# A fused scan and feed-forward kernel: one weight transfer issued earlier, w_in's later pieces converted in another order

## The chip, the cores and the metric

The kernel runs on one core of one Trainium2 chip. The metric is device time of one execution in microseconds (us). The kernel before takes 349.14 us, the median of three runs (349.01 to 349.2).

## What is computed

A chunked state-space scan (Mamba-2) on 4 batches, 8 heads, 768 positions, head size 32 and state size 16; its output, reshaped to 3072 tokens of 256 values, goes through a feed-forward block of width 2048 with the quick GELU:

```python
for c in range(nc):                      # chunks of the sequence, per batch and head
    cum = np.cumsum(log(a)[chunk])
    y[chunk] = (C @ B.T * exp(cum_i - cum_j) * causal) @ x   # within the chunk
             + (C @ state) * exp(cum)                        # from the chunks before
    state = exp(sum(log a)) * state + (B * exp(cum_end - cum)).T @ x
h = y.reshape(3072, 256) @ w_in          # 256 x 2048
g = h / (1 + exp(-1.702 * h))
out = g @ w_out                          # 2048 x 256
```

x, a, B and C are 32-bit numbers. w_in and w_out arrive in 64-bit floating point and are converted on the chip, from their bits.

## The kernel before, in words

The tokens are worked off in six groups of 512 (`g` 0 to 5). A group has two pairs of chunks (pairs 0 and 1 for group 0, 2 and 3 for group 1). For group 0 the plain products are used: 16 calls of `hidden(0, f)`, f = 0 to 15, each two products on TensorE of w_in's block f with yT (the scan's output turned, halves k = 0 and 1) into one bank of PSUM `h`, and one Silu on ScalarE that reads the bank into gT. Then `project_all(0)` runs f = 0 to 15 again, two products each of w_out's block f with gT into the banks `o`. From group 1 on the products are made with a seven-product scheme (lines L948, L958, L1053, L1060) whose steps are written out by hand; the change does not touch it.

The order on each engine is the order in which the program calls the helpers (`in_order`, L21, keeps it). While group 0 is in `hidden` and `project_all`, the lists `in_hidden[0]` and `in_project[0]` (L1221 to L1253) name, for a place f, what is emitted right behind `hidden(0, f)`, or ahead of f in `project_all`. So place 8 of `in_hidden[0]` stands behind the Silu of f = 8 on ScalarE, and ahead of that of f = 9.

**The weights' way.** They come in ten pieces (`PIECES`, L154): pieces 0 to 3 hold two blocks of w_in each, pieces 4 and 5 four blocks each (8 to 11 and 12 to 15), pieces 6 to 9 four blocks of w_out each. A piece is transferred by `fetch` (two DMAs on SP's queue) into one of four buffers `bits`; pieces 0 and 1 share a buffer, 2 and 3 too. It is converted in four steps:

- `fields(i)`: two VectorE instructions (L192, L195) cut exponent (`p`, written p2 in the code) and mantissa (`m`) out of the upper words,
- `clamp(i)`: two ScalarE instructions (L203, L204) on `p`, which need the first of `fields`,
- `rounded(i)`: one VectorE instruction (L208) adds the lower words to `m`,
- `join(i, parts)`: two VectorE instructions per part (L222, which needs `clamp`, and L228), the last of which writes w_in or w_out.

`narrow(i)` emits rounded(i), fields(i + 1), join(i), all on VectorE. `join` also fetches a later piece: behind piece 1 comes piece 6, behind piece 5 piece 9 (`NEXT`).

**Beside it** VectorE, ScalarE and TensorE prepare the scan of pairs 2 and 3. `store_a` at place 5 clips the decays az on VectorE (L353, L357, L358) and stores them. `pick_a` at place 6 makes X from az by two ScalarE instructions (L366). `fan_all` at place 9 spreads X by 16 small products into PSUM and then runs four VectorE scans (L450) and two products Be (L461); with it a bank `rows4` is written (L501, L530), which `since_fanned` reads on VectorE (L541, L543). The banks of `h`, `rows4`, the turned B and C (`tp`) and `o` come from one pool of four, so a product waits until the bank's last reader is done. In `project_all`, places 0 and 2 turn B and C of pairs 2 and 3 (`turn`, L597, L590, and CsT, L667); place 9 makes scores, state increments (`gain`, L713) and states; `finish` adds the part of the earlier states (`inter`, L824, at place 13) and the part within the chunk (`intra`, L838, at place 15) into PSUM and copies it to yT of group 1 (L871).

**The start.** SP issues a, B, piece 0 and the four DMAs of x for pairs 0 and 1. Piece 1 is held: GpSimd writes one element of its buffer (L171) after it has made CsT of pair 0, and SP's queue waits for that. Pieces 1 to 5 and az follow on SP's queue. A ninth DMA waits for the landing of the one eight earlier (eight semaphores are used in turn). `finish(range(PG))` runs the 128 products `intra` of pairs 0 and 1, a filling product `dense(4)`, then `inter` by halves t, each followed by its two ScalarE copies to yT (L856).

Of the kernel before, what the change touches and what calls it, by code (L numbers as in the profile page):

```python
# [35 lines left out]
def kernel(  # L36
# [31 lines left out]
    nc = tc.nc  # L68
# [69 lines left out]
    def load(p, parts=None):  # L138
        if parts is None:
            parts = "bcx" if p < 2 * PG else "bx"  # L140
            if p >= 2 * PG:
                load_blocks(p)
        for part in parts:
            dst, src, e = {"b": (rb, B, N), "c": (rc, C, N), "x": (rx, x, D)}[part]
            dst[p] = raw.tile([P, 2, NH, e], FP32, tag=part, name=f"{part}{p}",
                              bufs=2 if part == "c" else 3)
            for k in range(2):
                b, c = divmod(2 * p + k, NC)
                sl = slice(c * P, (c + 1) * P)
                nc.sync.dma_start(out=dst[p][:, k], in_=src[b, :, sl, :].rearrange("h s d -> s h d"))  # L150
# [55 lines left out]
    def rounded(i):  # L206

        nc.vector.scalar_tensor_tensor(out=mantissa[i].bitcast(FP32), in0=bits[i][0],  # L208
                                       scalar=2.0 ** -32, in1=mantissa[i],
                                       op0=ALU.mult, op1=ALU.add)  # L210
# [4 lines left out]
    def join(i, parts=1):  # L215

        name, f, n = PIECES[i]
        n //= parts
        low, m, p2 = bits.pop(i)[1], mantissa.pop(i), power.pop(i)
        for k in range(parts):  # L220
            cols, fs = slice(k * n * DM, (k + 1) * n * DM), slice(f + k * n, f + (k + 1) * n)
            nc.vector.scalar_tensor_tensor(out=p2[:, cols], in0=low[:, cols], scalar=0x80000000,  # L222
                                           in1=p2[:, cols], op0=ALU.bitwise_and, op1=ALU.bitwise_or)
            if name == "in":
                dst, h = w_in[:, fs].rearrange("p f k e -> p (f k e)").unsqueeze(1), 1
            else:
                dst, h = w_out[:, :, fs].rearrange("p c f e -> p c (f e)"), 2
            nc.vector.scalar_tensor_tensor(  # L228
                out=dst, in0=m[:, cols].bitcast(FP32).rearrange("p (h e) -> p h e", h=h),
                scalar=2.0 ** -20, in1=p2[:, cols].bitcast(FP32).rearrange("p (h e) -> p h e", h=h),  # L230
                op0=ALU.mult, op1=ALU.mult)
        for n in NEXT.get(i, ()):
            fetch(n)

    def narrow(i):
        rounded(i)
        if i + 1 < len(PIECES):
            fields(i + 1)
        join(i, 2 if i == 4 else 1)


    scratch = dram.tile([NC, 2, NB * NH, H], FP32, name="scratch")
# [47 lines left out]
    fetch(0)  # L290
    load(0, "x")
    load(1, "x")


    edge = const.tile([P, 2], FP32, name="edge")
# [84 lines left out]
    for i, n, head in ((0, 1, PG), (1, 2, PG), (0, 0, 1)):  # L380
        t = whose[32 * i:32 * i + 32, n:n + 1]
# [202 lines left out]
    def area(name):  # L584
        return psa.tile([P, R, 4 * P], FP32, tag="cb", name=name)
# [202 lines left out]
    def finish(pairs, steps=range(2)):  # L788


        g, first = divmod(pairs[0], PG)
        early = pairs[0] < PG

        swap = g > 2
        if 0 in steps:
            if early:
                y = [bank(f"y0_{i}")[:, :2 * P].rearrange("p (k i) -> p k i", i=H) for i in range(4)]
                begun_y[0] = [[y[2 * t + i] for t in range(NK)] for i in range(2)], set()
            else:
                both = area(f"y{pairs[0]}")[:, :, :len(pairs) * 2 * H].rearrange(  # L800
                    "p (s t) (k i) -> p s t k i", s=2, i=H)
                begun_y[pairs[0]] = [[both[:, i, t] for t in range(NK)] for i in range(2)] + [both], set()
        y, begun = begun_y[pairs[0]]

        def begin(i, t, parts):
            new = not begun & {(i, t, q) for q in parts}
            begun.update((i, t, q) for q in parts)
            return new

        def inter(n, p, ts=range(2)):  # L810

            for k in range(2):
                for i in range(2):
                    m = 2 * k + i
                    if (4 * p + m) % (2 * NC) == 0:
                        continue
                    old = state[p][:, m - 1] if m else state[p - 1][:, 3]
                    for r in range(R):
                        t = r // 2
                        if t not in ts:  # L820
                            continue
                        half = r % 2 ^ (swap and i)
                        rows, to = slice(32 * r, 32 * r + 32), Q * D * half
                        nc.tensor.matmul(  # L824
                            out=y[i][t][to:to + Q * D, 2 * n + k], lhsT=old[rows],
                            rhs=st[p]["CsT"][rows, k, SIDES[i]],
                            start=begin(i, t, range(Q * half, Q * half + Q)), stop=early,
                            tile_position=(32 * r, to), skip_group_check=True)

        def intra(n, p):  # L830
            L = Ls[p]
            for k in range(2):
                for h in range(NH):
                    for i, side in enumerate(SIDES):
                        t, q = divmod(h, HB)
                        if i and swap:
                            q = (q + Q) % HB
                        nc.tensor.matmul(  # L838
                            out=y[i][t][D * q:D * q + D, 2 * n + k], lhsT=rx[p][side, k, h],
                            rhs=L[side, k, h // Q, h % Q],  # L840
                            start=begin(i, t, (q,)), stop=not early, tile_position=(H * i, D * q),
                            skip_group_check=True)

        cols = slice(2 * first * P, 2 * (first + len(pairs)) * P)

        if first == 0:
            yT[g] = ffn.tile([P, NK, TG], FP32, tag="yT", name=f"yT{g}")
        if early:
            for n, p in enumerate(pairs):
                intra(n, p)  # L850
            dense(4, area("idle")[:, 0])
            for t in range(NK):
                for n, p in enumerate(pairs):
                    inter(n, p, (t,))
                for i in range(2):
                    nc.scalar.activation(  # L856
                        yT[g][:, t, cols].rearrange("p (k s i) -> p s k i", s=2, i=H)[:, i], y[i][t],
                        AF.Copy)
        else:
            for step in steps:  # L860
                for n, p in enumerate(pairs):
                    (inter, intra)[step](n, p)
            if 1 not in steps:
                return
            o = yT[g][:, :, cols].rearrange("p t (k s i) -> p s t k i", s=2, i=H)
            for i in range(2):
                if i and swap:
                    for to, src in (SIDES, SIDES[::-1]):
                        nc.scalar.activation(o[to, i], y[2][src, i], AF.Copy)
                else:  # L870
                    nc.scalar.activation(o[:, i], y[2][:, i], AF.Copy)  # L871
        for p in pairs:
            state.pop(p - 1, None)
            st.pop(p)
            Ls.pop(p)
# [287 lines left out]
    def dense(n, t):  # L1163
        nc.tensor.matmul(out=t[:, :n * H], lhsT=ones,
                         rhs=ones[:, :H].unsqueeze(1).to_broadcast([P, n, H]),
                         start=True, stop=True, skip_group_check=True)
# [27 lines left out]
    gain(range(PG))  # L1194
    parts_first()
    since_start(0, nc.gpsimd)
    fetch(1, held=nc.gpsimd)
    for i in range(2, 6):
        fetch(i)
    rows_a(az, (nc.sync,))  # L1200
    since_start(1, nc.gpsimd)
# [2 lines left out]
    dense(8, bank("dense"))  # L1204
    finish(range(PG))
    join(0, 2)
    fields(1)
    clamp(1)
    table(AF.Silu)
    rounded(1)  # L1210
    fold_ident(1)
    join(1)
    fields(2)
    clamp(2)
# [3 lines left out]
    def at(places, i, *work):  # L1218
        places.setdefault(i, []).extend(work)

    in_hidden = [{} for _ in range(NG)]  # L1221
    in_project = [{} for _ in range(NG)]
# [7 lines left out]
    at(in_hidden[0], 6, lambda: pick_a(PG))  # L1230
    at(in_hidden[0], 9, lambda: fan_all(PG))
    at(in_hidden[0], 9, since_fanned)
    for i, k, c in ((2, 1, 1), (3, 2, 2), (4, 4, 4), (5, 6, 8), (6, 9, 12), (7, 12, 15)):
        at(in_hidden[0], k, lambda i=i: narrow(i))
        at(in_hidden[0], c, lambda i=i: clamp(i + 1))
    at(in_hidden[0], 9, lambda: spread(PG + 1), lambda: spread_rows(1))
    n, p = 2 * PG, 3 * PG
    pairs = PG, PG + 1
# [5 lines left out]
    at(in_project[0], 5, lambda: narrow(9))  # L1244
    at(in_project[0], 9, lambda: score(pairs), lambda: gain(pairs), lambda: keep_both(pairs, True),
       lambda: weigh(PG), lambda: weigh(PG + 1))
    at(in_project[0], 13, lambda: finish(pairs, (0,)))
    at(in_project[0], 15, lambda: finish(pairs, (1,)))
    at(in_project[0], 13, lambda: mix_in(1), lambda: spread(n + 1, held=True),
       lambda: load(n + 1, "x"), lambda: mix_in(2), lambda: mix_in(3),  # L1250
       lambda: turn_blocks(2), lambda: decay(n))
# [197 lines left out]
```

## Time and profile before

| | |
|---|---|
| median of three runs | 349.14 us |
| the profiled execution, its own time | 350.11 us |
| its span in the trace | 348.0 us |
| TensorE busy | 342.8 us, 99% of the span |
| VectorE busy | 254.0 us, 73% |
| ScalarE busy | 155.2 us, 45% |
| granted TensorE clock | 1.00 |
| first product of `hidden(0, 0)` | 18.40 us |
| first product of `project_all(0)` | 48.90 us |
| first product of `hidden(1, 0)` | 82.07 us |

In the profile a line of the timeline gives start and length in us, the engine, the line of the code, the operation, out<-in, the shapes and a count; in brackets the idle time of the engine just before, and what ended it. PE is TensorE's products, PEld its weight loads, DVE VectorE, ACT ScalarE, POOL GpSimd, SPq the DMA queue on SyncE. Starts on one engine can overlap a little with the end of the instruction before. All of the change lies in the first 85 us.

### The profile page before, as it was taken

To read this page: it belongs to the slowest core of one execution; us is meant where nothing else is said; L and a number is where in the kernel's file an instruction comes from. 1 tells how busy PE (TensorE), PEld (TensorE's weight loads), DVE (VectorE), ACT (ScalarE), POOL (GpSimd) and SP (SyncE) were. 2 spreads that over 40 slices of the span, in tenths; PEclk is the share of its full clock that TensorE was granted. 3 is DMA by queue.
4 is the path that set the end of the run, shared out by engine and by line. 5 is a ranking of instruction groups with operands and counts; after the bars stand their busy time and mean duration, and the time that the engine had idled before them with its cause. 6 is when DMAs were issued, how large, how long until landed. Compare 5 with 4: busy or idle time off the path is not lost.

```text
span 348.0 us, 8123 instructions
## 1 busy us (share of the span) xinstructions
PE 342.8 (99%) x3380; PEld 269.6 (77%) x3380; DVE 254.0 (73%) x479; ACT 155.2 (45%) x352; POOL 13.1 (4%) x42
## 2 busy tenths in 40 slices
PE   8999999999999999999999999999999999999996
PEld 6643444545688888888888888888888888899996
DVE  5899997999779999667997567788465654465463
ACT  4798675106453322754442454432564331554320
POOL 8300000100000100000000000000000000000000
PEclk9999999999999999999999999999999999999999
DMA  6598899535526200436704036400000300000301
GB/s 161 128 329 190 199 211 225 104 62 99 109 45 132 62 0 2 77 70 117 120 16 61 0 66 116 81 0 3 0 4 3 59 4 0 0 2 0 62 0 61
DMA packets 89980, 25.92 MB, mean 74 GB/s; under 512 B 73432, under 2 KB 87128, under 8 KB 89944
## 3 DMA queue, kind: packets, MB, share of 16 engines
q1 hardware_dynamic: 89112, 24.88, 33.7%
q10 hardware_dynamic: 832, 0.52, 0.6%
q8 instruction: 26, 0.43, 0.5%
q14 instruction: 10, 0.08, 0.1%
HBM read 22.15 MB, written 3.24 MB: 73 GB/s over the span
## 4 chain that ended last, share of the span: by engine, by line
PE 83%; DMA 7%; DVE 5%; SPq 2%; issue 2%; POOL 0%; ACT 0%; DVEq 0%
PE acc L1053 28%; PE X L948 19%; PE Y L958 14%; PE acc L1060 7%; PE o L990 4%; DMA bits<-in_moe_w_in_dram 3%; DMA af<-in_a_dram 3%; PE h L893 2%; PE y L838 2%; SPq L180 2%; PE cb L682 2%; PE y L824 1%; PE A L713 1%; DVE p L222 1%; PE ab L554 1%
## 5 line engine op out<-in xcount | busy, mean ns | idle before, releaser
L953 ACT ACTIVATE ac<-X 128x256 f32<-128x256 f32 x76 | 29.1, 383 | 81.4 <-PE X L948 80.7
L1080 DVE TENSOR_TENSOR gT<-Y,ac 128x512 f32<-128x512 f32 x38 | 26.2, 689 | 40.3 <-PE Y L958 32.5
L1053 PE MATMUL acc<-mg,mw 128*128 128x256 f32 x192 | 54.5, 379 | 0.0
L925 ACT ACTIVATE gT<-gT 128x512 f32<-128x512 f32 (+1 forms) x76 | 38.9, 519 | 29.4 <-DVE gT L1080 28.9
L948 PE MATMUL X<-my,mi 128*128 128x256 f32 x152 | 45.2, 380 | 0.0
L1053 PEld LDWEIGHTS acc<-mg,mw 128*128 128x128 f32 x192 | 36.5, 190 | 5.0
L1080 DVE TENSOR_TENSOR gT<-Y,b 128x256 f32<-128x256 f32 x38 | 15.8, 418 | 28.5 <-PE Y L958 28.5
L893 PE MATMUL h<-yT,w_in 128*128 128x512 f32 x80 | 35.8, 598 | 0.5 <-DVE w_in L228 0.4
L1053 PE MATMUL acc<-gT,w_out 128*128 128x256 f32 x128 | 35.5, 379 | 0.0
L948 PEld LDWEIGHTS X<-my,mi 128*128 128x128 f32 x152 | 28.0, 190 | 4.1 <-ACT ac L953 0.4
L893 PEld LDWEIGHTS h<-yT,w_in 128*128 128x128 f32 x80 | 14.7, 190 | 19.2 <-issue 15.6
L990 PE MATMUL o<-gT,w_out 128*128 128x512 f32 x64 | 28.6, 597 | 0.0
L916 DVE TENSOR_TENSOR mg<-gT 128x512 f32<-128x512 f32 x40 | 27.2, 681 | 0.0
L1053 PEld LDWEIGHTS acc<-gT,w_out 128*128 128x128 f32 x128 | 24.2, 190 | 3.4 <-ACT yT L871 0.2
L953 ACT ACTIVATE b<-X 128x256 f32<-128x256 f32 x38 | 14.6, 384 | 21.0 <-PE X L948 20.5
L948 PE MATMUL X<-yT,w_in 128*128 128x256 f32 x76 | 23.2, 389 | 0.0
L958 PE MATMUL Y<-yT,w_in 128*128 128x256 f32 x76 | 22.7, 381 | 0.0
L958 PE MATMUL Y<-my,mi 128*128 128x256 f32 x76 | 22.7, 380 | 0.0
L958 PE MATMUL Y<-yT,mi 128*128 128x256 f32 x76 | 22.5, 379 | 0.0
L948 PE MATMUL X<-my,w_in 128*128 128x256 f32 x76 | 22.4, 379 | 0.0
L990 PEld LDWEIGHTS o<-gT,w_out 128*128 128x128 f32 x64 | 11.8, 190 | 13.2 <-issue 12.4
L402 DVE TENSOR_TENSOR_SCAN L<-a,idents 128x1024 f32<-128x1024 f32 x9 | 20.5, 2277 | 0.4 <-DMA a<-scratch 0.4
(159 smaller groups left out, 548.0 us busy)
## 6 DMA issues: line engine op xcount, KB each, us to landing
a<-scratch SPq DMA_DIRECT2D x18, 256.0 KB, 5.0
bits<-in_moe_w_out_dram SPq DMA_DIRECT2D x8, 512.0 KB, 5.7
x<-in_x_dram SPq DMA_DIRECT2D x24, 128.0 KB, 3.1
out_dram<-ob SPq DMA_DIRECT2D x40, 64.0 KB, 1.9
bits<-in_moe_w_in_dram SPq DMA_DIRECT2D x8, 256.0 KB, 4.7
bits<-in_moe_w_in_dram SPq DMA_DIRECT2D x4, 512.0 KB, 11.2
b<-in_B_dram SPq DMA_DIRECT2D x20, 64.0 KB, 3.1
af<-in_a_dram SPq DMA_DIRECT2D x3, 384.0 KB
```

Source lines behind the costliest of these rows:

```text
L180: nc.sync.dma_start(out=dst[k], in_=src[k])
L402: nc.vector.tensor_tensor_scan(out=L, data0=ra[p].rearrange("p k e -> p (k e)"), data1=idents.rearrange("p h i -> p (h i)"), initial=0.0, ...
L893: nc.tensor.matmul(out=h, lhsT=w_in[:, f, k], rhs=yT[g][:, k], start=(k == 0), stop=(k == NK - 1), skip_group_check=True)
L916: nc.vector.tensor_tensor(out=t[:, 0:2], in0=B[:, :, 1], in1=B[:, 0], op=ALU.subtract)
L925: nc.scalar.activation(o, i, AF.Silu, scale=GELU_SCALE)
L948: nc.tensor.matmul(out=s["X"], lhsT=lhsT, rhs=rhs, start=i == "1", stop=i == "4", skip_group_check=True)
L953: nc.scalar.activation(copy, s["X"], AF.Copy)
L958: nc.tensor.matmul(out=o, lhsT=lhsT, rhs=rhs, start=s.pop("new", False), stop=i != "5", skip_group_check=True)
L990: nc.tensor.matmul(out=o[c], lhsT=w_out[:, c, f], rhs=gT[g, f // 2][:, f % 2], start=(f == 0), stop=(f == NF - 1), skip_group_check=True)
L1053: nc.tensor.matmul(out=acc[g][0][i][:, cols], lhsT=w, rhs=h[:, cols], start=(j == 0 and k == 0 and (i, 0) in begins), stop=(j == NF // 2 - ...
L1060: nc.tensor.matmul(out=o[k] if type(o) is list else o[:, cols], lhsT=h[:, cols], rhs=w, start=(j == 0 and (i, k) in begins), stop=(j == NF ...
L1080: nc.vector.tensor_tensor(out=o, in0=v, in1=w, op=ALU.add)
```

## The change

1. Piece 1 (w_in's blocks 2 and 3) is fetched directly behind the last x at the start, without hold; GpSimd's hold now stands before piece 2.
2. The initial `finish` runs `inter` by sides i (the chunk's two halves) with all four row groups in turn, instead of by t, and the four copies come behind; the filling product is `dense(3)` instead of `dense(4)`.
3. `fold_ident(1)` (one VectorE instruction, L335) moves from behind `rounded(1)` to ahead of `fields(1)`.
4. In `narrow`, pieces 4 and 5 are joined, in two parts each, ahead of the next piece's `fields`. Before, `fields` came first, and piece 5 was joined in one part.
5. Places in `in_hidden[0]`: clamp(5) from place 4 to 8, narrow(5) from 6 to 8, clamp(6) from 8 to 11, narrow(6) from 9 to 11, clamp(7) stays at 12.
6. `finish(pairs)` in `project_all(0)` stands whole at place 15; before, its `inter` was at place 13.

```diff
     def narrow(i):
         rounded(i)
+        if i in (4, 5):
+            join(i, 2)
         if i + 1 < len(PIECES):
             fields(i + 1)
-        join(i, 2 if i == 4 else 1)
+        if i not in (4, 5):
+            join(i)
...
     load(1, "x")
+    fetch(1)
...
-        def inter(n, p, ts=range(2)):
+        def inter(n, p, sides=range(2)):
             for k in range(2):
-                for i in range(2):
+                for i in sides:
...
-                        if t not in ts:
-                            continue
...
-            dense(4, area("idle")[:, 0])
+            dense(3, area("idle")[:, 0])
+            for i in range(2):
+                for n, p in enumerate(pairs):
+                    inter(n, p, (i,))
             for t in range(NK):
-                for n, p in enumerate(pairs):
-                    inter(n, p, (t,))
...
-    fetch(1, held=nc.gpsimd)
-    for i in range(2, 6):
+    fetch(2, held=nc.gpsimd)
+    for i in range(3, 6):
         fetch(i)
...
     join(0, 2)
+    fold_ident(1)
     fields(1)
     clamp(1)
     table(AF.Silu)
     rounded(1)
-    fold_ident(1)
     join(1)
...
-    for i, k, c in ((2, 1, 1), (3, 2, 2), (4, 4, 4), (5, 6, 8), (6, 9, 12), (7, 12, 15)):
+    for i, k, c in ((2, 1, 1), (3, 2, 2), (4, 4, 8), (5, 8, 11), (6, 11, 12), (7, 12, 15)):
         at(in_hidden[0], k, lambda i=i: narrow(i))
         at(in_hidden[0], c, lambda i=i: clamp(i + 1))
...
-    at(in_project[0], 13, lambda: finish(pairs, (0,)))
-    at(in_project[0], 15, lambda: finish(pairs, (1,)))
+    at(in_project[0], 15, lambda: finish(pairs))
```

## The prediction

> **What bounds the kernel now.** I read the page's busy shares first (PE 342.8 of 348.0 us), then the timeline of PE, DVE and ACT from 15 to 95 us, since the change touches nothing behind `hidden(1, 1)`, and last the landings of the DMAs. TensorE is full from 18.40 us on: a step f of `hidden` or `project_all` takes four weight loads and products 0.43 us apart, 1.714 us. So a microsecond is won or lost only where PE stands. The PE timeline:
>
> ```profile
> 18.40 14.26 PE L893 MATMUL h<-yT,w_in 128*128 128x512 f32 x32
> 33.10 3.67 PE L893 MATMUL h<-yT,w_in 128*128 128x512 f32 x8 [0.45 <-DVE w_in L228]
> 36.70 0.69 PE L412 MATMUL ab<-X,ones 32*64 32x256 f32 x16
> ...
> 38.06 10.57 PE L893 MATMUL h<-yT,w_in 128*128 128x512 f32 x24
> ...
> 48.90 3.60 PE L990 MATMUL o<-gT,w_out 128*128 128x512 f32 x8
> ```
>
> Only f = 8 waits visibly: its first product stands at 33.10, the last one before it at 32.06, so 0.61 us beyond the pace, and 0.08 for the restart. Inside the first line f = 2 waits too (22.11 instead of 21.93, and the restart: 0.26). Both wait for w_in from VectorE, whose timeline is full:
>
> ```profile
> 30.33 0.69 DVE L192 TENSOR_SCALAR p<-bits 128x1024 uint32<-128x1024 uint32 x1 [0.67 <-DMA bits<-in_moe_w_in_dram]
> 30.94 0.69 DVE L195 TENSOR_SCALAR m<-bits 128x1024 uint32<-128x1024 uint32 x1
> 31.54 0.69 DVE L222 SCALAR_TENSOR_TENSOR p<-bits,p 128x512 uint32<-128x512 uint32 x1
> 32.26 0.69 DVE L228 SCALAR_TENSOR_TENSOR w_in<-m,p 128x512 f32<-128x512 f32 x1
> ...
> 34.20 0.55 DVE L353 TENSOR_SCALAR az<-az 128x768 f32<-128x768 f32 x1
> ...
> 39.74 2.43 DVE L450 TENSOR_TENSOR_SCAN L<-ab,idents 128x256 f32<-128x256 f32 x4
> ...
> 46.98 1.23 DVE L228 SCALAR_TENSOR_TENSOR w_out<-m,p 128x1024 f32<-128x1024 f32 x1
> ```
>
> The reader sees VectorE wait for piece 5 (0.67 us) before it may join piece 4, and that w_out's first blocks are done at 48.21, just 0.69 us before PE takes them at 48.90. This small reserve decides the case. ScalarE in the same stretch:
>
> ```profile
> 31.06 1.15 ACT L203 ACTIVATE p<-p,edge 128x1024 f32<-128x1024 uint32 x1 [1.13 <-DVE p L192]
> ...
> 35.19 0.91 ACT L366 ACTIVATE X<-az,pick 128x256 f32<-128x256 f32 x2 [0.83 <-issue]
> 36.00 1.06 ACT L896 ACTIVATE gT<-h 128x512 f32<-128x512 f32 x2
> 36.95 1.15 ACT L203 ACTIVATE p<-p,edge 128x1024 f32<-128x1024 uint32 x1
> 38.13 1.15 ACT L204 ACTIVATE p<-p,edge 128x1024 uint32<-128x1024 f32 x1
> ```
>
> Clamp(5) runs at 31.06, long before piece 5 is joined. X waits for az (its last VectorE instruction ends at 35.10).
>
> **The start (parts 1 to 3).** dense(3) has 192 columns a product instead of 256 and ends 0.16 us earlier (two products, 0.32 apart). `inter` by sides lets four row groups run side by side: the row at 74.23 is that form, 56 products in 1.04 us, against 1.68 here. It begins at 16.58, ends near 17.7; the two copies that f = 0 needs then end near 18.07 (0.32 us each) instead of 18.35, and f = 0 starts at 18.12, 0.28 earlier. It wants blocks 2 and 3 at 21.65. VectorE ends join(0) at 17.85 as before; then comes `fold_ident` (17.77, next start 0.61 later), fields(1) at 18.38 instead of 18.46, clamp(1) on ScalarE at 18.84 instead of 18.92, ending 20.32; join(1) follows at 20.39 instead of 20.56 (before, the fold stood in front). So f = 2 starts at 21.94, not 22.11: a gain of 0.17 us. The early piece 1 takes away a DMA wait of 0.61 us, and the fold, formerly hidden behind clamp(1), fills it.
>
> Piece 1 off the queue at 12.72 moves pieces 2 to 5 one place up: piece 2 lands by about 18.4 (where piece 1 did), piece 5 some 2.4 us earlier than its 30.21. VectorE needs them at 21.7, 23.1, 25.7 and 32.1: no DMA wait is left. New is that piece 1's 512 KB stand right behind x in the same queue. The second half of x for pair 1 lands at 12.15, its products L713 run from 12.4. Bounds: nothing (x goes first) or one such transfer's spacing, 1.36 us (landings of pieces 4 and 5), less 0.3 of reserve: 1.0 us. I take nothing, as x is issued first on the same queue. The Trainium skill, "DMA: Bandwidth & Descriptors", HWDGE ordering, says each engine takes descriptors in ring order, yet a later one may finish its write before an earlier one: by it, the sum stays between the same ends.
>
> **Pieces 4 and 5 (parts 4, 5).** VectorE now starts rounded(4) at 28.28 and join(4) at 29.39 (1.11 later; clamp(4), at 28.80, is done). First half ready at 30.8, f = 8 wants it at 32.31: the wait goes, and f = 8 runs 0.79 earlier. Up to f = 9 PE has gained 0.9 us (X products at 35.8 instead of 36.70).
>
> Then it turns. VectorE: second half of join(4) 30.72 and 31.44, fields(5) 32.05, az clip 33.25 instead of 34.20, rounded(5) 34.06 to 35.27. Now join(5) needs clamp(5), which stands on ScalarE behind X and the Silus of f = 7 and 8. X starts when az is done, 34.24; clamp(5) starts 1.76 later, as at 35.19 and 36.95 above: 36.00, its second at 37.18, end 38.33. VectorE idles from 35.27 to 38.38, **3.1 us**, and behind the waiting join(5) are queued fields(6), the scans, since_fanned, and w_out's first piece. From 38.38: four instructions of join(5) (0.61 + 0.72 + 0.61 + 0.72, two parts cost 0.25 more than one) to 41.04; fields(6) 1.20 to 42.24; from the first scan to w_out ready took 39.74 to 48.21, 8.47 us: **50.7** instead of 48.21. Blocks 12 and 14 are ready at 39.8 and 41.1, PE wants them at 40.6 and 44.0: in time. The bank of `rows4` is read until 46.0; f = 15, whose bank it becomes, wants it at 45.8: 0.35 lost. PE would reach `project_all` at 48.36 and starts it at 50.83 (0.14 behind the last write, as at 22.11), with 0.08 for the restart: **2.0 us later than before**. ScalarE points the same way: its clamp(7) waits for fields(7), 47.7, and holds the Silus of f = 13 to 15 until 50.56 to 51.7; `o` takes the banks of 13 and 14.
>
> **Given back (part 6 and the stage behind).** VectorE after this is 0.7 us late (fields(9) at 57.3 instead of 56.65, where it waited 1.75 us for a DMA, now earlier), PE 2.0. So PE waits no more for CsT of pair 3, in front of `gain` (PE row at 66.02, gap near 66.46): 0.35 back. `inter` and `intra` in one go save one change between big and small products: 0.09 + 0.08 + 0.10 beyond the pace at 74.23, 75.20 and 75.74, less 0.05 between the two: 0.22 back. Bits9 and the spread of pair 3 are fetched behind join(5) and join(6), 41.0 and 49.5; SP issued them at 48.72 and 50.02, so they cost nothing.
>
> **Sum**: 2.01 - 0.35 - 0.22 = 1.4 us slower. The profiled execution (350.11, of which 348.0 is span) would become 351.5; it stands 0.97 above the median, so the median goes from 349.14 to **350.5 us**.
>
> **Rivals.**
> 1. *Faster: the reserve holds.* If VectorE's idle time at join(5) is under 0.6 us instead of 3.1, w_out's first blocks come before PE wants them; the 0.9 of f = 2 and f = 8 and the 0.22 stay: 348.0 us. For it: VectorE is ahead by 0.95 there. Against: clamp(5)'s place behind X, whose 1.76 us are on the ScalarE rows. 0.12.
> 2. *About even*: half the idle time (an X or a Silu earlier than its row says) leaves PE waiting 1 us less, 349.2 to 349.8. 0.15.
> 3. *x late* behind the unheld piece 1: the whole start shifts up to 1.0: 351.5. Speaks for it: 0.3 us of reserve only. 0.07.
> 4. *The clock falls* while PE idles 2.5 us before `project_all`. In the first rows eight products of 192 columns took 2.93 us, 0.37 each, against 0.16 at the later pace (0.43 x 192/512), and full pace shows between 5.8 and 7.7 us: some 6 us at half speed cost 3: 353.5. No idle time before is over 0.61, so the trace can't say at which it falls. The Trainium skill, "TensorE: Matmul & The Clock Gate", What's actually happening, lets the clock halve after an idle window of about 3.4 us and return after as long a busy one; estimated by it, a fall would cost 1.7 us, and 2.5 us is short of it. 0.06.
>
> The forecast itself (350.0 to 351.1) has 0.60.
>
> **Range and chances.** 348.9 to 352.0 takes in the forecast, the even case and x late (1.0 above); left out are rival 1 and most of 4. A measurement here tells 0.2% (0.7 us) from nothing: below 348.44 is 0.12, up to 349.84 0.16 (rival 2 and a little of the forecast), above 0.72.
>
> **What would show it.** Right: DVE idle about 3 us before L222 of piece 5, released by ACT L204; PE idle about 2.5 us before the first L990, near 50.8; no wait at f = 8; f = 2 still waiting, near 21.9; X at 34.2. Wrong: w_out L228 done before 49, PE's first L990 before 48.9, a late L713 at the start, or a clock under 1.0 behind 50 us.

## The result, and the profile after

The changed kernel takes **352.92 us** (median of six runs, 351.61 to 355.08) against 349.16 us for the kernel before beside it (six runs, 348.61 to 349.44): ratio 1.0115, 95% interval 1.008 to 1.015. It is slower, by more than the 1.4 us forecast and beyond the range.

The runs of before lie within 1 us, those of after within 3.5 us, and the granted clock sorts them. It was 1.000 in 351.61, 352.00 and 352.69, 0.995 in 353.15, and 0.990 in 354.16 and 355.08. A deficit of 0.005 over 350 us is some 1.75 us of lost time. No run of before was under 0.999. The profiled execution (352.00 us, span 349.9) is one of full clock, so its trace shows the change without the clock's part. The PE timeline of after, from the start to group 1 (start and length in us, engine, line, operation, shapes, count, and in brackets the idle time before and what ended it; lines stand three or four lower than before):

```profile
13.64 1.07 PE L840 MATMUL y<-L,x 64*32 64x64 f32 x75
15.98 0.76 PE L840 MATMUL y<-L,x 64*32 64x64 f32 x53 [1.27 <-issue]
...
17.19 1.04 PE L826 MATMUL y<-CsT,S 32*64 32x64 f32 x56
18.70 17.48 PE L896 MATMUL h<-yT,w_in 128*128 128x512 f32 x40 [0.47 <-ACT yT L859]
36.12 0.69 PE L416 MATMUL ab<-X,ones 32*64 32x256 f32 x16
...
51.16 3.67 PE L993 MATMUL o<-gT,w_out 128*128 128x512 f32 x8 [2.33 <-DVE w_out L228]
...
79.57 1.04 PE L826 MATMUL y<-CsT,S 32*64 32x64 f32 x56
80.54 1.49 PE L840 MATMUL y<-L,x 64*32 64x64 f32 x128
...
83.78 3.60 PE L896 MATMUL h<-yT,w_in 128*128 128x512 f32 x8
```

The wait at f = 8 is gone (forty products of `hidden` in one line), X is spread at 36.12 instead of 36.70, and then PE stands 2.33 us ahead of `project_all`, for w_out. Not expected is the first bracket: 1.27 us in the middle of the intra products, with no releaser. VectorE's timeline of after shows where w_out lost its time:

```profile
33.56 0.55 DVE L357 TENSOR_SCALAR az<-az 128x768 f32<-128x768 f32 x1
...
38.67 0.69 DVE L222 SCALAR_TENSOR_TENSOR p<-bits,p 128x512 uint32<-128x512 uint32 x1 [3.09 <-ACT p L204]
...
42.54 2.42 DVE L454 TENSOR_TENSOR_SCAN L<-ab,idents 128x256 f32<-128x256 f32 x4
...
49.78 1.22 DVE L228 SCALAR_TENSOR_TENSOR w_out<-m,p 128x1024 f32<-128x1024 f32 x1
```

and ScalarE's what VectorE waited for:

```profile
34.55 0.91 ACT L370 ACTIVATE X<-az,pick 128x256 f32<-128x256 f32 x2 [2.87 <-DMA c<-in_C_dram]
35.36 1.06 ACT L899 ACTIVATE gT<-h 128x512 f32<-128x512 f32 x2
36.31 1.15 ACT L203 ACTIVATE p<-p,edge 128x1024 f32<-128x1024 uint32 x1
37.49 1.15 ACT L204 ACTIVATE p<-p,edge 128x1024 uint32<-128x1024 f32 x1
```

ScalarE takes X and two Silus first, then the two instructions of clamp(5). They end at 38.64, join(5) starts at 38.67, and all that is queued on VectorE behind join(5) is late: w_out's first blocks are ready at 51.00 instead of 48.21. The 2.87 us of idle ScalarE ahead of X are free time in which clamp(5) could have run, had it stood there.

The part that the prediction worked out, from the first product of `hidden(0, 0)` to that of `hidden(1, 0)`, went from 63.67 to 65.08 us: **+1.41**. The rest of the loss lies elsewhere.

### The profile page after: what moved, and what is told of

Read it like the earlier page. It is cut to its first block, busy times and chain, and to the rows that moved or that the text cites. A ratio compares the mean times of both kernels' runs of the same rounds, so it can differ in the third digit from the quotient of the medians.

```text
span 349.9 us, 8125 instructions
## 1 busy us (share of the span) xinstructions
PE 341.3 (98%) x3380; PEld 268.6 (77%) x3380; DVE 254.4 (73%) x481; ACT 154.9 (44%) x352; POOL 13.1 (4%) x42
## 4 chain that ended last, share of the span: by engine, by line
PE 79%; DVE 7%; DMA 7%; SPq 2%; ACT 1%; issue 1%; POOL 0%; ACTq 0%; DVEq 0%; POOLq 0%
PE acc L1056 25%; PE X L951 17%; PE Y L961 13%; PE o L993 8%; PE acc L1063 7%; DMA bits<-in_moe_w_in_dram 3%; PE h L896 2%; PE cb L686 2%; PE y L840 2%; DMA a<-scratch 1%; PE y L826 1%; SPq L180 1%; PE A L717 1%; SPq L150 1%; DMA c<-in_C_dram 1%
```

## The experiments

All medians are of runs beside runs of the kernel before on the same chip (349.02 us, 23 runs, for the first four kernels; 348.98, 21 runs, for the next four; 348.98, 17 runs, for the last three). Kernel 3's run of 354.94 us, with a granted clock of 0.985, counts in its median and not in its ratio. "Full clock" counts runs with a granted clock of 0.999 or more, "PE stands" is the wait ahead of `project_all(0)` in the profile.

| kernel | median us | ratio (95%) | full clock | median of those | PE stands |
|---|---|---|---|---|---|
| after | 352.92 | 1.0115 (1.008 to 1.015) | 3 of 6 | 352.00 | 2.33 |
| 1 clamp early | 349.29 | 1.0023 (1.0002 to 1.0045) | 10 of 12 | 349.13 | 0 |
| 2 hold back | 352.86 | 1.0112 (1.0087 to 1.0138) | 3 of 6 | 350.74 | 2.32 |
| 3 fetch alone | 349.01 | 1.0003 (0.9988 to 1.0018) | 10 of 11 | 348.93 | 0 |
| 4 fill | 351.78 | 1.0093 (1.0074 to 1.0112) | 5 of 6 | 351.69 | filled |
| 5 hold and fill | 351.83 | 1.0073 (1.0044 to 1.0102) | 7 of 7 | 351.83 | filled |
| 6 longer wait | 355.40 | 1.0192 (1.0155 to 1.0229) | 0 of 6 | | 4.38 |
| 7 hold and clamp | 349.02 | 1.0001 (0.9981 to 1.002) | 12 of 12 | 349.02 | 0 |
| 8 pieces alone | 352.26 | 1.0093 (1.0063 to 1.0122) | 5 of 9 | 351.57 | 2.32 |
| 9 wait and one | 353.53 | 1.0134 (1.0109 to 1.016) | 1 of 4 | 352.65 | 2.93 |
| 10 short fill | 351.46 | 1.0073 (1.0055 to 1.0092) | 6 of 6 | 351.46 | 1.46 |
| 11 spread later | 348.39 | 0.9994 (0.9976 to 1.0012) | 12 of 12 | 348.39 | 0 |

**1. clamp(5) at place 5 instead of 8.** The theory: its place behind X is what makes w_out late.

```diff
-    ... (4, 4, 8), (5, 8, 11), (6, 11, 12), (7, 12, 15)):
+    ... (4, 4, 5), (5, 8, 11), (6, 11, 12), (7, 12, 15)):
```

> The changed kernel with clamp(5) moved from place 8 to place 5 of in_hidden[0] (ahead of X on ScalarE); nothing else. Theory W (VectorE waits for clamp(5), and PE for w_out behind it): DVE's idle time of 3.09 us ahead of L222 of piece 5 falls under 0.5, PE's wait of 2.33 us ahead of the first L993 goes; X comes about 1.4 us later (behind the clamp) and costs PE about 0.8 us ahead of the spread of X: 349.3 us, between 348.7 and 350.0. Theory G (without the long wait PE's clock cannot fall): every run within 0.3% of the others and a granted clock of 1.00 in each. Theory F (the unheld piece 1 is what costs): still 352 or more.

One number takes away 3.6 of the 3.76 us. The waits of VectorE and PE are gone from its trace: the last turn product stands at 51.47, the first `o` at 51.69. But 10 runs lie at 348.24 to 349.88 and two at 352.07 and 352.20 with a clock of 0.990, and the profile is the former of these two. Its PE rows at the start, and its table of stretches (length; busy time of PE, PEld, DVE, ACT, POOL; granted clock; DMA share; GB/s):

```profile
13.68 1.21 PE L840 MATMUL y<-L,x 64*32 64x64 f32 x75
16.44 0.76 PE L840 MATMUL y<-L,x 64*32 64x64 f32 x53 [1.55 <-issue]
```

```profile
14.67:17.25 2.58, 1.03 (x77) 0.78 (x62) 2.50 (x6) 1.51 (x3) 0.00 (x0) 1.00 0.93 308
17.26:24.08 6.82, 6.35 (x63) 3.66 (x64) 4.33 (x9) 4.30 (x9) 0.00 (x0) 0.50 0.92 286
24.09:39.50 15.41, 15.41 (x38) 6.53 (x37) 15.01 (x26) 12.57 (x19) 0.00 (x0) 1.00 0.83 175
```

A stand of 1.55 us in the intra products, which is in the first stretch, is followed by 6.82 us at half clock.

**2. Piece 1 held again** (the early fetch undone, all else as in after).

```diff
-    fetch(1)
...
-    fetch(2, held=nc.gpsimd)
-    for i in range(3, 6):
+    fetch(1, held=nc.gpsimd)
+    for i in range(2, 6):
```

> The changed kernel with piece 1 held again by GpSimd, as before; the rest of the change stays. Theory F (piece 1 behind x delays the block of PE's instructions and with it the products L840 at the start): the gap of 1.27 us in L840 shrinks to the 0.4 us of before, hidden(0, 0) starts near 18.1 instead of 18.70; if that cost the kernel its time, 350 us or less. Theory W: f = 2 is bound by VectorE in both, so the end stays, PE's wait ahead of the first L993 is still 2 us or more: 351.5 to 352.5 in runs with a clock of 1.00. Theory G: some of the runs again show a clock under 1.00 and 353 us or more.

The median does not move (352.86 against 352.92), and three of six runs have lost clock here too, all at 0.995. So the early fetch is not what makes most of the loss. The full-clock runs alone are lower than in after, 350.35, 350.74 and 352.83 against 351.61 to 352.69, and partly under the 351.5 expected; three runs each, which overlap. In the trace `hidden(0, 0)` starts at 17.36 instead of 18.70.

**3. The early fetch alone, in the kernel before.**

```diff
     load(1, "x")
+    fetch(1)
...
-    fetch(1, held=nc.gpsimd)
-    for i in range(2, 6):
+    fetch(2, held=nc.gpsimd)
+    for i in range(3, 6):
```

> The kernel before with nothing but piece 1 fetched directly behind the last x (the hold now ahead of piece 2). Theory F: the gap in L838 at the start grows from 0.38 to 1.0 us or more, the first hidden comes 0.5 us later, near 18.9; piece 5 lands earlier, so that its wait of 0.67 us on VectorE goes; together 349.2 us, between 348.8 and 349.8. If piece 1 delays nothing at the start: 348.5, f = 0 at 18.4 and no wait of PE at f = 8. Theories W and G: no wait of PE over 1 us and no clock under 1.00 in either case.

No difference in the median. Its PE rows:

```profile
16.22 0.76 PE L839 MATMUL y<-L,x 64*32 64x64 f32 x53 [1.34 <-issue]
19.21 17.56 PE L894 MATMUL h<-yT,w_in 128*128 128x512 f32 x40
...
48.90 3.60 PE L991 MATMUL o<-gT,w_out 128*128 128x512 f32 x8
```

The null is made of two parts: PE stands in the intra products and starts `hidden` at 19.21 instead of 18.40, and the stretch from there to `hidden(1, 0)` is 62.43 us instead of 63.67, 0.81 of the difference in `hidden`, where f = 2 and f = 8 no longer wait, and 0.43 in `project_all`, ahead of `gain`.

**4 and 5. PE kept at work while it waits**: three pairs of filling products into a spare bank ahead of `project_all`, in after (4), and in after with piece 1 held (5).

```diff
+    def fill(n):
+        t = area("fill")
+        for i in range(n):
+            dense(8, t[:, i % R])
+
-    at(in_project[0], 0, lambda: turn(PG), lambda: rounded(8),
+    at(in_project[0], 0, lambda: turn(PG), lambda: fill(3), lambda: rounded(8),
```

> The changed kernel with three filling products of 512 columns (ones by ones, about 0.86 us each) into a spare area of PSUM, emitted on TensorE behind the turned B and C of pair 2 and ahead of project_all's f = 0, where PE otherwise stands 2.33 us. The fill's result is not used. Theory G (PE's clock falls in some executions because PE stands there): the clock is 1.00 in all runs, and all lie between 351.5 and 352.5. If the spread of the changed kernel (351.6 to 355.1) has another cause, it stays: runs over 353.5 with a clock under 1.00. Theory W: the first L993 still starts near 51.2.

> The changed kernel with piece 1 held again and with the three filling products ahead of project_all's f = 0 (their result is not used). Theory G2 (the clock falls at two places: two windows long behind the late instruction block at the start, which the hold prevents, one window long ahead of project_all, which the fill prevents): no run under a clock of 0.999, all between 350.2 and 351.8, the spread under 1.2 us. If the falls have another cause: again some runs over 352.5 with a clock of 0.995 or 0.99.

The PE rows of 4 show that the products fill the wait and no more:

```profile
48.36 2.74 PE L1167 MATMUL fill<-ones 128*128 128x512 f32 x6
50.94 3.60 PE L993 MATMUL o<-gT,w_out 128*128 128x512 f32 x8
```

The useful work starts as late as in after (50.94 against 51.16), and yet the median falls by 1.1 us, and 12 of 13 runs keep the full clock, where 6 of 12 of after and kernel 2 did. Part of the loss is therefore not the wait itself but what the idle PE does to the clock. One run of 4 at 0.995 stays unexplained, and the runs of 5 spread over 1.38 us, a little more than the 1.2 expected.

**6. A longer wait**: three more VectorE instructions of 0.6 us each ahead of w_out.

```diff
+    at(in_hidden[0], 10, *[lambda: fold_ident(1)] * 3)
```

> The changed kernel with three more VectorE instructions of 0.69 us (fold_ident(1) written again, the same values) at place 10, ahead of w_out's first piece. Theory W: each 0.61 us on VectorE goes straight to PE: its wait ahead of the first L993 grows from 2.3 to about 4.1 us, 353.6 us where the clock stays. Theory G: a wait longer than one window of 3.4 us lets the clock fall in every run: clock 0.995 or less in nearly all, 355 us or more, and the profile shows 0.50 for 3.4 us or more behind the wait. If the wait does not move the clock: 353 to 354.2 and a clock of 1.00 in most.

All six runs lose clock (three at 0.995, three at 0.990). Its profile holds a fall: the PE row of the first `o`, and the table of stretches before it and from it on.

```profile
52.47 5.37 PE L993 MATMUL o<-gT,w_out 128*128 128x512 f32 x8 [4.38 <-DVE w_out L228]
```

```profile
48.10:52.83 4.73, 0.36 (x1) 0.30 (x2) 4.70 (x6) 3.44 (x5) 0.00 (x0) 1.00 0.85 246
52.83:56.24 3.41, 3.41 (x5) 1.35 (x4) 3.38 (x5) 2.44 (x3) 0.00 (x0) 0.50 0.82 144
```

The clock is 0.50 for 3.41 us just behind the wait, when PE is busy again. Eight products took 5.37 us where after takes 3.67: 1.70 us. That is the price of one fall, and 0.005 of 350 us.

**7. Hold back and clamp(5) at place 5** (edits 1 and 2 together).

> The changed kernel with clamp(5) at place 5 instead of 8 and with piece 1 held as before: both suspected causes undone, the rest (inter by sides, pieces 4 and 5 joined ahead, finish in one go, fold ahead) kept. Theories W and F together: no wait ahead of project_all, no late instruction block, PE waits only at f = 2 (about 0.3 us); 0.7 us or more faster than the kernel before: 348.1, between 347.5 and 348.7, clock 1.00 in all. If the rest of the change cost time as well: 349 or more.

349.02: even with before, all 12 runs at full clock, and not the gain expected. Its PE rows tell why:

```profile
36.29 0.69 PE L415 MATMUL ab<-X,ones 32*64 32x256 f32 x16 [0.70 <-ACT X L369]
...
48.49 3.60 PE L992 MATMUL o<-gT,w_out 128*128 128x512 f32 x8
```

With clamp(5) ahead of X on ScalarE, PE waits 0.70 us for X instead: `project_all` starts 30.95 us after `hidden`, 0.45 more than before.

**8. Only the order of pieces 4 and 5** (parts 4 and 5 of the change) in the kernel before.

```diff
     def narrow(i):
         rounded(i)
+        if i in (4, 5):
+            join(i, 2)
         if i + 1 < len(PIECES):
             fields(i + 1)
-        join(i, 2 if i == 4 else 1)
+        if i not in (4, 5):
+            join(i)
...
-    ... (4, 4, 4), (5, 6, 8), (6, 9, 12), (7, 12, 15)):
+    ... (4, 4, 8), (5, 8, 11), (6, 11, 12), (7, 12, 15)):
```

> The kernel before with nothing but the other order and places of pieces 4 and 5 (join ahead of fields, clamp(5) at place 8 and what goes with it). Theory W: the whole lasting loss comes with this part: DVE waits about 3 us for clamp(5), PE about 2.3 us ahead of the first product of project_all; 351.2 us in runs with a clock of 1.00, between 350.4 and 351.8. Theory G: some runs at 0.995 and 1.7 us longer. If this part alone does nothing: 349.

This alone gives nearly the whole loss, 352.26 us, with the same waits; of VectorE's and PE's rows of it:

```profile
38.96 0.69 DVE L222 SCALAR_TENSOR_TENSOR p<-bits,p 128x512 uint32<-128x512 uint32 x1 [3.09 <-ACT p L204]
```

```profile
51.44 3.67 PE L993 MATMUL o<-gT,w_out 128*128 128x512 f32 x8 [2.32 <-DVE w_out L228]
```

Four of nine runs lost clock.

**9 and 10. The wait made a little longer and shorter**, both with piece 1 held: one `fold_ident(1)` at place 10 (9), or one pair of filling products instead of three (10).

> The changed kernel with piece 1 held again and one more VectorE instruction of 0.69 us (fold_ident(1) once more, the same values) at place 10: PE's wait ahead of project_all grows from 2.3 to 2.9 us. Theory G (the clock falls by the length of the wait, with a chance that grows up to one window): falls in more runs than the half seen at 2.3 us, in fewer than all, 0.995 each; runs at full clock near 351.5, the others near 353.2; if the profiled run is one of them, the profile shows 0.50 for about 3.4 us just behind the wait. If the length does not matter: the same half as at 2.3 us.

> The changed kernel with piece 1 held again and one filling product of 512 columns (0.86 us, result not used) instead of three ahead of project_all's f = 0: PE stands for about 1.5 us instead of 2.3. Theory G: falls become rare, at most 1 run in 6 under 0.999, median near 351.3. If any wait at this place tips the clock: half of the runs at 0.995 and 353 us, as without the fill.

PE stood 2.93 us in 9, and three of four runs lost one window of clock; it stood 1.46 us in 10, and none of six did. The PE row of 9, and below it those of 10:

```profile
52.16 3.67 PE L992 MATMUL o<-gT,w_out 128*128 128x512 f32 x8 [2.93 <-DVE w_out L228]
```

```profile
48.11 1.02 PE L1166 MATMUL fill<-ones 128*128 128x512 f32 x2
50.60 3.67 PE L992 MATMUL o<-gT,w_out 128*128 128x512 f32 x8 [1.46 <-DVE w_out L228]
```

**11. As 7, and X spread at place 10 instead of 9**, to take away the wait for X.

```diff
-    at(in_hidden[0], 9, lambda: fan_all(PG))
-    at(in_hidden[0], 9, since_fanned)
+    at(in_hidden[0], 10, lambda: fan_all(PG))
+    at(in_hidden[0], 10, since_fanned)
```

> The changed kernel with piece 1 held, clamp(5) at place 5, and the spread of X with since_fanned at place 10 instead of 9. With clamp(5) early alone PE still stood 0.86 us for X ahead of the spread; a place later X is in time. Theory W: that wait goes and nothing takes its place, since VectorE reaches the scans later than the spread in either case: 348.2, between 347.6 and 348.7, faster than the kernel before by 0.8. If VectorE or w_out's first piece becomes late instead: 349.0 as with clamp(5) early alone.

`project_all` starts 30.02 us after `hidden`, 0.48 less than before. But the ratio's interval holds 1, so no gain over before is shown. PE and VectorE of 11, behind that:

```profile
64.50 0.30 PE L716 MATMUL A<-x,Be 64*32 64x64 f32 x2
66.38 0.78 PE L716 MATMUL A<-x,Be 64*32 64x64 f32 x54 [1.58 <-DVE CsT L670]
```

```profile
64.01 1.76 DVE L496 TENSOR_TENSOR_SCAN since<-af,first 128x768 f32<-128x768 f32 x1 [0.55 <-POOL af L489]
65.90 0.42 DVE L670 TENSOR_TENSOR CsT<-tp,since 128x256 f32<-128x256 f32 x1
```

What was won goes in the next wait: the state products of pair 3 now stand 1.58 us for VectorE's CsT, and `hidden(0, 0)` to `hidden(1, 0)` takes 64.43 us, 0.76 more than before. That the median came near the expected 348.2 is therefore luck: the expectation had nothing in that wait's place.

## Why the prediction was wrong

**Point by point.** Most steps of the stretch that the prediction worked out held:

| step | forecast | measured |
|---|---|---|
| VectorE idle at join(5), for clamp(5) | 3.1 | 3.09 |
| X on ScalarE starts | 34.24 | 34.55 |
| spread of X, no wait at f = 8 | 35.8 | 36.12, none |
| PE idle ahead of `project_all` | 2.5 | 2.33 |
| first product of `project_all` | 50.83 | 51.16 |
| first product of `hidden(0, 0)` | 18.12 | 18.70 |
| `hidden(0, 0)` to `hidden(1, 0)` (1.4 + 0.28 more) | +1.7 | +1.41 |
| f = 2 (wanted 21.65) | starts at 21.94 | no wait, f = 0 came late |
| `finish` in one go, no wait for CsT | yes | yes (79.57) |

The mechanism is shown, not only argued: kernel 8 has these two parts of the change alone and the loss, kernel 1 undoes one number of them and the loss goes. The sign and the main term were right. Two terms failed.

**First, the clock: "2.5 us is short of it. 0.06."** This step weighed rival 4 wrongly. The runs, ordered by how long PE stood ahead of `project_all`, give this; the kernels with the early piece 1 stand apart, since the clock can also fall at their start, as in the trace of 1:

| PE stands, us | piece 1 | kernels | runs that lost clock |
|---|---|---|---|
| 0, or filled | held | 5, 7, 11 | 0 of 31 |
| 1.46 | held | 10 | 0 of 6 |
| 2.3 | held | 2, 8 | 7 of 15 |
| 2.93 | held | 9 | 3 of 4 |
| 0, or filled | early | 1, 3, 4 | 4 of 29 |
| 2.33 | early | after | 3 of 6 |
| 4.38 | early | 6 | 6 of 6 |

The falls go with the wait, from none at 1.46 us to all at 4.38; the four runs at 2.93 can't be told from the fifteen at 2.3. About half of the runs behind a wait of 2.3 us lose one stretch of 3.41 us at half rate, 1.7 us, some two. That moves the median of after from 352.00 (full clock alone) to 352.92, and spreads its runs. The Trainium skill, "TensorE: Matmul & The Clock Gate", What's actually happening, says that the clock halves after an idle window of about 3.4 us, counted on a clock that runs freely, and comes back after a busy one. The length of the fall agrees with it (3.41 and 6.82 us at 0.50, one window and two). That a gap must be as long as a window before it costs anything does not: 2.3 us were enough in 7 of 15 runs. I used the page as a threshold where it gives a price. Where in time after's own falls lie is inferred from this series and from kernels 4, 5 and 10; only the falls of 1 and 6 are in a trace, and by the early row of the table some of after's may lie at the start.

The traces hint at why one wait costs clock in half of the runs. In the ten traces that record changes of the granted clock, whole steps of 3.413 us lie between them: in kernel 6 the clock is recorded as full from 5.04 us and as half from 52.83, 14 steps later; in kernel 1 it is full from 7.02 and half from 17.26, 3 steps later. Laid over the waits, the edges of these steps cut them: in the full-clock profiles of after, 2, 8 and 9 no one step holds more than 1.72 us of idle TensorE, while in 6 the step just ahead of the fall holds 3.05. A wait of 2.3 us would then cost clock or not by where an edge happens to cut it. This fits, but no run set the place of the edges, and idle time alone doesn't decide: in kernel 1 the step ahead of the fall holds only 1.61 us, beside small products.

**Second, the start and the profile's offset.** The prediction took 0.28 us off the start ("I take nothing" for the early piece) and carried the 0.97 us by which the profiled execution of before stood above its median over to after. Neither held. In the trace of after, `hidden(0, 0)` starts 0.30 later. From the first score product on it is 0.70 later (9.00 us against 8.30), and that product stood 0.40 earlier. And after's profiled execution stands not above but at the median of its full-clock runs. If executions of a kernel differ only ahead of `hidden`, the typical start is the profile's, moved by the median minus the profiled time: 18.40 - 0.95 = 17.45 for before and 18.70 for after, **1.25 later**. This is an estimate by that assumption, from three full-clock runs of after. Of the 2.84 us at full clock (352.00 less 349.16) this is 1.25, `hidden(0, 0)` to `hidden(1, 0)` 1.41, and 0.19 lie behind it.

PE's rows of the start in before (compare the first two rows of after, above):

```profile
13.82 1.21 PE L838 MATMUL y<-L,x 64*32 64x64 f32 x75
15.40 0.76 PE L838 MATMUL y<-L,x 64*32 64x64 f32 x53 [0.38 <-issue]
```

In every kernel that stands there it does so behind the same product, the 75th. Shortly before, the trace has one packet of 16,384 bytes on a queue named "instruction". It ends at 13.95 in before and at 14.74 in after; PE goes on 1.45 and 1.24 us later; in before, after and kernels 1 to 10 it is 1.21 to 1.46 us. The DMA view of the two stretches around it, busy share of the DMA engines in 40 slices and the packets of that queue (number, MB, share), before first (12.8 to 14.2 us), then after (13.5 to 15):

```profile
DMA  0000900000000000000000000009550656699996
...
q8 instruction: 1, 0.02, 4.4%
```

```profile
DMA  3384339939494335356696676976966787795696
...
q8 instruction: 1, 0.02, 3.9%
```

In before the block comes for the most part while the hold keeps the data transfers back; in after it shares the engines with piece 1. It is no slower for that, 0.94 us against 0.99; it starts later, at 13.80 instead of 12.96. The same split runs through all traces: the block starts at 13.07 to 13.96 us in the five kernels with the early piece and at 12.29 to 12.96 in the eight with the hold. PE's stand (the bracket of that row) was 0.69 to 1.55 us in the five, and none to 0.67 us in seven of the eight; the eighth, kernel 8, stood 1.09 us, and there the block took 1.62 us. Rival 3 (x late, up to 1.0) had about the right size and the wrong carrier: x landed as before (12.27 against 12.15).

What this costs in the medians is less clear, for the three pairs that differ in the hold alone do not agree. Kernel 3 against before: the traced stretch is 1.24 us shorter and the median the same, so about 1.2 us are lost ahead of it. After against 2: at full clock 352.00 and 350.74. Kernels 4 and 5: 351.69 and 351.83 at full clock, no cost. By the subtraction above the typical starts of the held kernels 2, 5, 7, 8, 10 and 11 also lie far apart, 16.5 (11) to 18.3 us (8), so it is a rough measure. Why the block starts later behind piece 1, and how much of the start's 1.25 us is due to it, **stays open**. What is shown is that undoing the early fetch alone does not bring the median back (2 against after, 5 against 4).

So of the 3.76 us, 1.41 are the forecast's own term (there 1.7 with the start put apart), 1.25, by the estimate above, the start where -0.28 was put, 0.19 small changes behind, and 0.92 the clock. The range failed by 0.92 us, as much as the clock's part alone.

## What to carry to other kernels

When a step is moved behind others, price the queue it joins: one place in ScalarE's order cost 3.1 us of VectorE and, through everything queued there, 2.3 us of TensorE. A wait of the bounding engine has a second price that a single profile at full clock hides: here a TensorE gap of over 2 us cost another 1.7 us in half of the runs, so read the clock of every run, and test by filling the gap with products. And a profiled execution's distance from its kernel's median is no constant to be carried over.

## What the runs showed of the hardware

- TensorE's clock fell behind gaps well under its 3.41 us window: in 0 of 6 runs at 1.46 us, 7 of 15 at 2.3 us, 3 of 4 at 2.93 us; behind 4.38 us it fell in 6 of 6. In the ten traces that record its changes, they lie whole steps of 3.413 us apart (14 steps in kernel 6, 3 in kernel 1). At the start, 1.55 us of standing in the midst of small products was followed by two windows at half clock (kernel 1).
- TensorE stood up to 1.55 us at the same product of its instruction stream, 1.2 to 1.5 us behind the landing of a 16,384-byte packet on the "instruction" queue; the trace names no releaser, only "issue". That packet started at 13.07 us or later in the five kernels with the early transfer, and at 12.96 or earlier in the eight without. The Trainium skill, "Runtime: NRT & Kernel Launch", Instruction fetch mechanics, says that an engine's instructions are refilled in blocks of 16 KiB by its own DMA queue and that crossing a block's end is mostly hidden. The size agrees; hidden it is in one profile here (kernel 11), and in the other twelve TensorE stands 0.24 to 1.55 us.
- Executions of one kernel at full clock differ by up to 3 us (before: 347.96 to 351.03 over the runs beside the experiments).
